# Float64 weights as one 24-bit word cut into short pieces, and the layer change's operands made by GpSimd

## The chip, the cores and the metric

The kernel runs on one core of a Trainium2 chip. A core has a matrix engine (TensorE, "PE" in the profile, its weight loads "PEld"), VectorE (DVE), ScalarE (ACT), GpSimd (POOL) and a queue engine (SP) that issues the loads here. Each engine runs its own instructions strictly in order and waits for others by semaphores. The metric is the device time of one execution in microseconds; the time before is the median of three runs.

## What is computed

Three stages follow each other: clustered attention, a feed-forward layer with ELU (layer 1) and a layer of four weighted experts with ReLU (layer 2).

```python
def reference(**kwargs):
    ...
    attn_out = _attn_ref(**attn_kwargs)            # 2 x 8 heads, 768 x 64, mask from 16 clusters
    x = attn_out.transpose(0, 2, 1, 3).reshape(1536, 512)
    x = _moe_ref(x=x, **moe_kwargs)                # h = x @ w_in;  ELU;  @ w_out   (512 -> 2048 -> 512)
    return _moe2_ref(x=x, **moe2_kwargs)           # out += p[:, e] * (relu(x @ w1[e]) @ w2[e]), e = 0..3
```

`w_in` and `w_out` arrive as float64 (divided by a square root in numpy), so the kernel reads them as pairs of 32-bit integers. All products are made in split form: each operand is a high part `h` and a low part `l`, and a product is `h*h + h*l + l*h`.

## The kernel before

**Attention** (the first 277 us) is a software pipeline written out by hand: the table `AT` gives each piece of work a time within a period, and sorting by time gives the order on every engine. The piece `W0` runs one step of `weights(n)`, which splits the float64 weights of chunks 0 and 1 of layer 1 in four halves (128x512, temporaries `w_tmp`), one step per period.

**Layer 1** has 16 weight chunks of 128 hidden features. A step is one chunk on one block of 512 tokens, so there are 48 steps (0 to 47), in groups of 2, 4, 5 and 5 chunks, each group over the three token blocks. In step s the main loop emits `tick(2s)`, then `emit_G1(s+2)` (12 matmuls from `xT` into PSUM `h`, then ACT relu and exp on L755 and L756, DVE `gg` on L757, POOL `gh` and `gl` on L758 and L759), then `tick(2s+1)`, then `emit_G2(s)` (12 matmuls on L869 into four PSUM banks `a`, of which there are five). Where a group closes (steps 1, 3, 5, 9, 13, 17, 22 and so on) the banks are moved into `acc` by ACT (L885, the first group) or added by DVE (L887). The next step's second bank can only be written when the first has been evicted. `tick` runs one piece (one `yield`) of each generator in `going`. The generator `w_split(n)` turns the float64 pair of chunk n (tile `st`) into `wh` and `wl`, starting at tick 4(n-2)-4 for chunks 2 to 14, so there is one chunk per two steps. Before, it has 7 DVE operations (L698, L702, L705, L709, L712, L717, L722), 2 of ACT (L701, L716) and one of POOL (L724, the last, which gives `wl`). Its temporaries are `wc` (two places in turn), `wql` and `wkh` (one place each, used by every chunk). Chunk 5 is first used by G1(9), the last first use of its group.

**Layer 2** has 16 chunks (16 to 31), 48 steps (48 to 95) and a Strassen-like product: `quad_early` makes five of seven products (the PSUM tile `px` is evicted by ACT on L779, L782 and L786 between its uses), then the first quarter of G2 of the step before, then `quad_late`, then the rest of G2. Its left operands are made by `x2_make` for each token block when layer 1 closes that block: four sums by DVE (`xs` on L828, L832, L838, L842) and seven splits, each an ACT copy (L645) and a subtraction by DVE (L648) or POOL (L650). Its right operands are made by `w2_split`: four differences `T` on DVE (L660 to L664) and five splits. The **layer change** is steps 47 to 51: block 2 closes in step 47, block 2's operands are first used by `quad_early(50)`, and chunk 17's by `quad_early(51)`. In the kernel before `ready` finishes a generator at the last moment, in front of the `quad_early` that needs it.

Of the kernel before, what the change touches and what calls it, by code (L numbers as in the profile page):

```python
# [46 lines left out]
def kernel(  # L47
# [56 lines left out]
    def attention():  # L104
# [379 lines left out]
        def weights(n):  # L484

            for i in range(2):
                raw = cv_p.tile([128, 512, 2], I32, tag="raw", name="w_raw")
                w_load(n, [raw], i)
                yield
                yield  # L490
                tmp = cv_p.tile([128, 3, 512], I32, tag="tmp", name="w_tmp")
                yield from w_split(n, [tmp[:, x] for x in range(3)], i)
# [159 lines left out]
    def w2_split(n):  # L652
# [3 lines left out]
        tags = W2_TAGS[n % 2]  # L656
        a = a.rearrange("p (k c f) -> p k c f", k=KD, c=2)
# [9 lines left out]
        for x, names in (  # L667
            (a[:, :, 0], ("B11", "B21")), (t[:, 0:2].rearrange("p a k f -> p (a k) f"), ("T1", "T2")),
            (t[:, 2:4].rearrange("p a k f -> p (a k) f"), ("T3", "T4")), (b22, ("B22",)),
        ):  # L670
            m = 2 * len(names)
            o = home(tags[len(ops) // 2], [128, 2, m, 128], "w1op")
            yield from split(o[:, 0], o[:, 1], x, dve)
            for i, nm in enumerate(names):
                ops[nm] = [[o[:, z, 2 * i + kk] for kk in range(2)] for z in range(2)]
            yield
        h, l = (home(tag, [128, 2, 512], "w2op") for tag in tags[4:])
        b = b.rearrange("p (c d) -> p c d", c=2)
        yield from split(h, l, b, dve)
# [3 lines left out]
    def w_split(n, tmp=None, half=None):  # L683
# [9 lines left out]

        small = tmp is not None
        c = tmp[0] if small else gtile(("qh", "kl")[n % 2], "wc", [128, 2, 512], I32)
        at = (slice(None),) * (len(a.shape) - 1)
        hi, lo = a[at + (1,)], a[at + (0,)]
        dve.tensor_scalar(c.bitcast(F32), hi.bitcast(F32), TOP, -TOP, ALU.min, ALU.max)  # L698
        yield
        b, s = tmp[1:] if small else [gtile(t, "w" + t, [128, 2, 512], I32) for t in ("ql", "kh")]  # L700
        act.activation(out=s.bitcast(F32), in_=c.bitcast(F32), func=AF.Abs)  # L701
        dve.tensor_scalar(b, c, 0x07FFFE00, 3, ALU.bitwise_and, ALU.logical_shift_left)  # L702
        if small:
            yield
        dve.scalar_tensor_tensor(  # L705
            out=b, in0=c, scalar=0xC0000000 - 2 ** 32, in1=b, op0=ALU.bitwise_and, op1=ALU.bitwise_or
        )
        yield
        dve.tensor_scalar(c, hi, 0x1FF, 23, ALU.bitwise_and, ALU.logical_shift_left)  # L709
        if small:  # L710
            yield
        dve.scalar_tensor_tensor(  # L712
            out=c, in0=lo, scalar=9, in1=c, op0=ALU.logical_shift_right, op1=ALU.bitwise_or
        )
        yield
        act.activation(out=c.bitcast(F32), in_=c.bitcast(U32), func=AF.Copy, scale=2.0 ** -43)  # L716
        dve.scalar_tensor_tensor(  # L717
            out=h, in0=s.bitcast(F32), scalar=LOW, in1=b.bitcast(F32), op0=ALU.is_ge, op1=ALU.mult
        )
        if small:  # L720
            yield
        dve.tensor_scalar(b, h.bitcast(I32), 0xFF800000 - 2 ** 32, None, ALU.bitwise_and)  # L722
        yield
        pool.tensor_tensor(l, c.bitcast(F32), b.bitcast(F32), ALU.mult)  # L724
        yield

    def moe():
# [84 lines left out]
        def x2_make(tb, t):  # L812
# [5 lines left out]
            def made(i, x):  # L818
                o = home(X2_TAGS[tb][i], [128, 2, 2, 256], "x2")
                x2[tb][i] = o[:, 0], o[:, 1]  # L820
                for _ in split(o[:, 0], o[:, 1], x, dve if i in (S1, S2, S4) else pool):
                    pass
# [89 lines left out]
        for n in range(W0, NC1):  # L912
            k = 5
# [6 lines left out]
        for n in range(NC1, NC1 + NP):  # L920
# [3 lines left out]
            else:  # L924
                t = 2 * (NS1 + NB * (i - 1)) + (1 if i > 1 else 2)
# [22 lines left out]
        for s in range(-LAG, NS):  # L948
# [11 lines left out]
            if s < NS1:  # L960
                tick(2 * s + 1)
            if s >= 0:
                emit_G2(s, (0,) if q else range(4))
            if q:
                quad_late(nxt, *q)
                if s >= NS1:
                    tick(2 * s, 3)
                    tick(2 * s + 1, 2)
# [37 lines left out]
```

## Time and profile before

| what | value |
|---|---|
| median of 3 runs | 1081.84 us (1081.2 to 1084.7) |
| profiled execution, its own time | 1085.26 us |
| its span, first to last instruction | 1083.4 us |
| PE busy | 1042.8 us (96%), 6253 matmuls |
| DVE, ACT, POOL busy | 781.2 us (72%), 495.3 us (46%), 396.7 us (37%) |
| attention | 0 to 276.9 us |
| layer 1 up to the first product of layer 2 | 276.9 to 557.4 us |
| layer change and layer 2 | 557.4 to 1083.4 us |
| granted TensorE clock, mean | 0.986 of full |

The shares are averages over stages with different limits: in attention DVE is busy for 95% of the time, in layer 2 for some 65%, and GpSimd does nothing in layer 2. PE's busy time contains stretches at half clock, and matmul ends are modelled, so a stage is judged by the pace of its steps and by PE's waits.

### The profile page before, as it was taken

Reading aid. Unit: us, or ns where it says so; the run is one execution under the profiler, and the core shown is the slowest. Engines: PE = TensorE matmul, PEld = TensorE weight load, DVE = VectorE, ACT = ScalarE, POOL = GpSimd, SP = SyncE. Lnnn points to the kernel's source line nnn. Section 1 sums busy time; section 2 is a strip of 40 time slices with the busy share of each in tenths; the row PEclk is TensorE's granted clock in tenths of the full one; section 3 lists DMA queues with packets and bytes.
Section 4 is the critical chain, followed back from the end, with each engine's and each line's share of the span. In section 5 each row is a group of like instructions: output and inputs, shape, how many; then the busy total and the mean of one; then the engine's idle time right before and its main releaser. Section 6 shows DMA issues by size and latency. Waiting matters only on the chain.

```text
span 1083.4 us, 16478 instructions
## 1 busy us (share of the span) xinstructions
PE 1042.8 (96%) x6253; PEld 927.2 (86%) x6253; DVE 781.2 (72%) x1305; ACT 495.3 (46%) x1045; POOL 396.7 (37%) x391
## 2 busy tenths in 40 slices
PE   8999999999988898999998999999999999999998
PEld 7989999988776776888887889899998989899997
DVE  6899999898788998342666676766566676666665
ACT  4888888888354333232434233333223333323331
POOL 2788788889666666453651000000000000000000
PEclk9899999999999999999999999999999999999999
DMA  8746554431123222110010111110111110011003
GB/s 182 171 106 154 139 133 107 108 89 51 67 82 113 79 78 78 39 39 1 1 39 1 39 40 40 39 39 2 39 40 40 40 40 20 20 40 40 1 1 117
DMA packets 61790, 67.53 MB, mean 62 GB/s; under 512 B 29008, under 2 KB 47440, under 8 KB 61712
## 3 DMA queue, kind: packets, MB, share of 16 engines
q1 hardware_dynamic: 61712, 66.49, 21.7%
q8 instruction: 49, 0.80, 0.3%
q14 instruction: 29, 0.24, 0.1%
HBM read 43.08 MB, written 3.15 MB: 43 GB/s over the span
## 4 chain that ended last, share of the span: by engine, by line
PE 61%; DVE 10%; POOL 5%; issue 2%; ACT 2%; POOLq 0%; DVEq 0%; ACTq 0%
PE a L869 30%; PE h L768 22%; PE h L748 6%; POOL wl L724 2%; DVE wql L705 2%; POOL gh L758 1%; PE x L441 1%; DVE wc L712 1%; DVE wql L702 1%; DVE wc L709 1%; DVE acc L887 1%; DVE gg L757 1%; PE tps L412 1%; POOL gl L759 1%; DVE wc L698 0%
## 5 line engine op out<-in xcount | busy, mean ns | idle before, releaser
L768 PEld LDWEIGHTS h<-x,w1op 128*128 128x128 f32 x2016 | 258.2, 191 | 14.9 <-ACT r L779 3.8
L768 PE MATMUL h<-x,w1op 128*128 128x256 f32 x2016 | 262.4, 285 | 5.2 <-ACT r L779 3.6
L869 PE MATMUL a<-w2op,gh 128*128 128x512 f32 x768 | 239.0, 392 | 0.0
L869 PEld LDWEIGHTS a<-w2op,gh 128*128 128x128 f32 x768 | 138.6, 189 | 24.0
L878 DVE SCALAR_TENSOR_TENSOR acc<-a,prob,acc 128x512 f32<-128x512 f32 x180 | 129.7, 746 | 40.2 <-PE a L869 40.2
L869 PE MATMUL a<-w2op,gl 128*128 128x512 f32 x384 | 150.1, 391 | 0.0
L748 PE MATMUL h<-xT,wh 128*128 128x512 f32 x384 | 120.3, 395 | 0.0
L400 POOL TENSOR_SCALAR p<-e,sm 128x768 f32<-128x768 f32 x96 | 90.4, 949 | 42.5 <-DVE sm L394 24.0
L373 DVE TENSOR_REDUCE nm<-s 128x1 f32<-128x768 f32 x96 | 90.8, 945 | 4.9 <-PE s L367 4.9
L869 PE MATMUL a<-gh,wh 128*128 128x512 f32 x192 | 76.8, 400 | 14.2 <-DVE acc L887 9.9
L382 ACT ACTIVATE e<-s,nm 128x768 f32<-128x768 f32 x96 | 86.7, 903 | 8.0 <-POOL p L400 6.1
L412 PE MATMUL tps<-ident,p 128*128 128x128 f32 x576 | 85.8, 280 | 3.6 <-DVE pl L433 3.1
L748 PEld LDWEIGHTS h<-xT,wh 128*128 128x128 f32 x384 | 73.6, 192 | 15.6
L869 PEld LDWEIGHTS a<-w2op,gl 128*128 128x128 f32 x384 | 72.3, 188 | 15.7
L758 POOL TENSOR_SCALAR gh<-gg 128x512 fp32r<-128x512 f32 x48 | 45.9, 956 | 108.6 <-DVE gg L757 102.5
L433 DVE TENSOR_TENSOR pl<-tps,ph 128x512 fp32r<-128x512 f32 x112 | 76.0, 682 | 6.0 <-ACT ph L425 5.4
L757 DVE SCALAR_TENSOR_TENSOR gg<-r,h 128x512 f32<-128x512 f32 x48 | 32.7, 681 | 65.4 <-ACT r L756 48.5
L779 ACT ACTIVATE r<-h 128x256 f32<-128x256 f32 x48 | 18.4, 384 | 131.6 <-PE h L768 131.6
L441 PE MATMUL x<-ph,v 128*128 128x256 f32 x288 | 76.7, 298 | 1.4 <-DVE xs L461 1.3
L748 PE MATMUL h<-xT,wl 128*128 128x512 f32 x192 | 75.5, 393 | 2.2 <-POOL wl L724 2.2
L869 PE MATMUL a<-gl,wh 128*128 128x512 f32 x192 | 76.3, 398 | 0.0
L869 PE MATMUL a<-gh,wl 128*128 128x512 f32 x192 | 76.2, 397 | 0.0
(152 smaller groups left out, 1916.3 us busy)
## 6 DMA issues: line engine op xcount, KB each, us to landing
st<-in_moe_w_dram SPq DMA_DIRECT2D x32, 512.0 KB, 4.3
st<-in_moe_w_in_dram SPq DMA_DIRECT2D x14, 512.0 KB, 3.8
st<-in_moe_w_out_dram SPq DMA_DIRECT2D x14, 512.0 KB, 4.6
QA<-qh SPq DMA_DIRECT2D x32, 192.0 KB, 3.9
nq<-in_q_dram SPq DMA_DIRECT2D x16, 192.0 KB, 3.8
nk<-in_k_dram SPq DMA_DIRECT2D x16, 192.0 KB, 3.8
nv<-in_v_dram SPq DMA_DIRECT2D x8, 384.0 KB, 4.0
QB<-ql SPq DMA_DIRECT2D x16, 192.0 KB, 3.8
```

The costliest lines, as they stand in the source:

```text
L373: dve.tensor_reduce(out=m_t[w][:, i:i + 1], in_=s_t[HALF * w + i][:, :, 0:384], axis=AX.XY, op=ALU.max, negate=True)
L382: act.activation(out=e, in_=s_t.pop(u)[:, :, 0:384], func=AF.Exp, bias=m_t[w][:, i:i + 1], accum_out=e_t[w][0][:, i:i + 1])
L400: pool.tensor_scalar(p, e_t[w][1 + i].rearrange("p a b -> p (a b)"), e_t[w][0][:, i:i + 1], 1.0, ALU.mult, ALU.mult)
L412: pe.transpose(ps[:, x, :], p_t[w][i][:, c * 128:(c + 1) * 128], ident)
L433: dve.tensor_tensor(out=l, in0=ps, in1=h.bitcast(F32), op=ALU.subtract)
L441: pe.matmul(x_t[w], lhsT=v2[j][:, r, c, :], rhs=t[:, :, c, :], start=(c == 0 and t is ph[w]), stop=(c == T - 1 and t is pl[w]),)
L748: pe.matmul(ps, lhsT=w[:, 0, f], rhs=x, start=(kk == 0 and i == 0), stop=(kk == KD - 1 and i == 2))
L757: dve.scalar_tensor_tensor(out=gg, in0=r, scalar=-1.0, in1=ps, op0=ALU.add, op1=ALU.max)
L758: pool.tensor_scalar(gh, gg, 1.0, 0.0, ALU.mult, ALU.add)
L768: pe.matmul(ps, lhsT=w[wz][kk], rhs=x[xz][:, kk], start=(start and kk + i == 0), stop=(stop and kk == 1 and i == 2), skip_group_check=True,)
L869: pe.matmul(ps, lhsT=x, rhs=y, start=(opens and i == 0), stop=(closes and i == len(ops) - 1))
L878: dve.scalar_tensor_tensor(out=t, in0=ps, scalar=pr, in1=t, op0=ALU.mult, op1=ALU.add)
```

## The change

`w_split` is written anew. The absolute value of the high word is taken by ACT, clamped between `LOW` and `TOP` by DVE, shifted by DVE, joined with three bits of the low word by DVE; ACT takes the sign of the high word and once more an absolute value (which clears the top bit), DVE multiplies by the sign; then an ACT copy gives `h` and a POOL subtraction gives `l`. That is 4 operations of DVE, 4 of ACT and 1 of POOL, in 6 ticks instead of 5 (8 steps in attention, as before). The temporaries are `wa` (two places in turn) and `wsg` (one place); nothing of it is read by POOL except `wa` and `wh`. `tick(2s+1)` now stands behind `emit_G2(s)`, so behind a group's evictions. At the layer change, block 2's seven splits and chunk 17's five are subtracted by POOL, four pieces of block 2's `x2_make` run right behind step 47, and chunk 17 starts two ticks earlier.

```diff
@@ weights (attention)
-                tmp = cv_p.tile([128, 3, 512], I32, tag="tmp", name="w_tmp")
-                yield from w_split(n, [tmp[:, x] for x in range(3)], i)
+                tmp = cv_p.tile([128, 2, 512], I32, tag="tmp", name="w_tmp")
+                yield from w_split(n, [tmp[:, x] for x in range(2)], i)
@@ w2_split
+        eng = pool if n == NC1 + 1 else dve
...
-            yield from split(o[:, 0], o[:, 1], x, dve)
+            yield from split(o[:, 0], o[:, 1], x, eng)
...
-        yield from split(h, l, b, dve)
+        yield from split(h, l, b, eng)
@@ w_split
-        c = tmp[0] if small else gtile(("qh", "kl")[n % 2], "wc", [128, 2, 512], I32)
+        a32, sg = tmp if small else [gtile(("qh", "kl")[n % 2], "wa", [128, 2, 512], I32), gtile("ql", "wsg", [128, 2, 512], I32)]
...
-        dve.tensor_scalar(c.bitcast(F32), hi.bitcast(F32), TOP, -TOP, ALU.min, ALU.max)
+        x, sg = a32.bitcast(F32), sg.bitcast(F32)
+        act.activation(out=x, in_=hi.bitcast(F32), func=AF.Abs)
         yield
-        b, s = tmp[1:] if small else [gtile(t, "w" + t, [128, 2, 512], I32) for t in ("ql", "kh")]
-        act.activation(out=s.bitcast(F32), in_=c.bitcast(F32), func=AF.Abs)
-        dve.tensor_scalar(b, c, 0x07FFFE00, 3, ALU.bitwise_and, ALU.logical_shift_left)
+        dve.tensor_scalar(x, x, LOW, TOP, ALU.max, ALU.min)
         if small:
             yield
+        dve.tensor_scalar(a32, a32, 3, 0x40000000, ALU.logical_shift_left, ALU.bitwise_xor)
+        act.activation(out=sg, in_=hi.bitcast(F32), func=AF.Sign)
+        yield
         dve.scalar_tensor_tensor(
-            out=b, in0=c, scalar=0xC0000000 - 2 ** 32, in1=b, op0=ALU.bitwise_and, op1=ALU.bitwise_or
+            out=a32, in0=lo, scalar=29, in1=a32, op0=ALU.logical_shift_right, op1=ALU.bitwise_or
         )
         yield
-        dve.tensor_scalar(c, hi, 0x1FF, 23, ALU.bitwise_and, ALU.logical_shift_left)
+        act.activation(out=x, in_=x, func=AF.Abs)
+        yield
+        dve.tensor_tensor(out=x, in0=x, in1=sg, op=ALU.mult)
+        yield
+        act.activation(out=h, in_=x, func=AF.Copy)
         if small:
             yield
-        dve.scalar_tensor_tensor(
-            out=c, in0=lo, scalar=9, in1=c, op0=ALU.logical_shift_right, op1=ALU.bitwise_or
-        )
-        yield
-        act.activation(out=c.bitcast(F32), in_=c.bitcast(U32), func=AF.Copy, scale=2.0 ** -43)
-        dve.scalar_tensor_tensor(
-            out=h, in0=s.bitcast(F32), scalar=LOW, in1=b.bitcast(F32), op0=ALU.is_ge, op1=ALU.mult
-        )
-        if small:
-            yield
-        dve.tensor_scalar(b, h.bitcast(I32), 0xFF800000 - 2 ** 32, None, ALU.bitwise_and)
-        yield
-        pool.tensor_tensor(l, c.bitcast(F32), b.bitcast(F32), ALU.mult)
+        pool.tensor_tensor(l, x, h.bitcast(F32), ALU.subtract)
         yield
@@ x2_make
-                for _ in split(o[:, 0], o[:, 1], x, dve if i in (S1, S2, S4) else pool):
+                for _ in split(o[:, 0], o[:, 1], x, dve if i in (S1, S2, S4) and tb < NB - 1 else pool):
@@ moe, the plan and the main loop
-            k = 5
+            k = 6
...
-                t = 2 * (NS1 + NB * (i - 1)) + (1 if i > 1 else 2)
+                t = 2 * (NS1 + NB * (i - 1)) + (i > 1)
...
-            if s < NS1:
-                tick(2 * s + 1)
             if s >= 0:
                 emit_G2(s, (0,) if q else range(4))
+            if s < NS1:
+                tick(2 * s + 1, 4 if s == NS1 - 1 else 1)
...
-                    tick(2 * s, 3)
+                    tick(2 * s, 4 if s == NS1 else 3)
```

**What moves on the engines.** First, VectorE in layer 1, over the two steps that one chunk takes. `gg` is a step's eviction; all else is the weights of a chunk (`wh4` is chunk 4's high part). Before:

```order
L757 SCALAR_TENSOR_TENSOR gg_4622<-r_4621,h_4606 128x512
L702 TENSOR_SCALAR wql_4628<-wc_4601 128x1024
L705 SCALAR_TENSOR_TENSOR wql_4628<-wc_4601,wql_4628 128x1024
L709 TENSOR_SCALAR wc_4601<-st_4508 128x1024
L712 SCALAR_TENSOR_TENSOR wc_4601<-st_4508,wc_4601 128x1024
L757 SCALAR_TENSOR_TENSOR gg_4668<-r_4667,h_4652 128x512
L717 SCALAR_TENSOR_TENSOR wh4_4599<-wkh_4629,wql_4628 128x1024
L722 TENSOR_SCALAR wql_4628<-wh4_4599 128x1024
L698 TENSOR_SCALAR wc_4696<-st_4603 128x1024
```

and now, for the same chunk:

```order
L755 SCALAR_TENSOR_TENSOR gg_4613<-r_4612,h_4597 128x512
L705 TENSOR_SCALAR wa_4591<-wa_4591 128x1024
L708 TENSOR_SCALAR wa_4591<-wa_4591 128x1024
L711 SCALAR_TENSOR_TENSOR wa_4591<-st_4501,wa_4591 128x1024
L755 SCALAR_TENSOR_TENSOR gg_4658<-r_4657,h_4642 128x512
L717 TENSOR_TENSOR wa_4591<-wa_4591,wsg_4592 128x1024
L755 SCALAR_TENSOR_TENSOR gg_4706<-r_4705,h_4690 128x512
```

Three of the seven operations are gone, and three stand behind one step's `gg` and one behind the next.

Second, GpSimd around step 8 of layer 1. `gh` and `gl` belong to a step's G1, and `wl5` is chunk 5's low part. Before, from G1(7)'s pair on:

```order
L758 TENSOR_SCALAR gh_4760<-gg_4763 128x512
L759 TENSOR_TENSOR gl_4761<-gg_4763,gh_4760 128x512
L724 TENSOR_TENSOR wl5_4695<-wc_4696,wql_4723 128x1024
L758 TENSOR_SCALAR gh_4809<-gg_4812 128x512
L759 TENSOR_TENSOR gl_4810<-gg_4812,gh_4809 128x512
L758 TENSOR_SCALAR gh_4854<-gg_4857 128x512
```

and now, again from G1(7)'s pair on:

```order
L756 TENSOR_SCALAR gh_4748<-gg_4751 128x512
L757 TENSOR_TENSOR gl_4749<-gg_4751,gh_4748 128x512
L756 TENSOR_SCALAR gh_4796<-gg_4799 128x512
L757 TENSOR_TENSOR gl_4797<-gg_4799,gh_4796 128x512
L722 TENSOR_TENSOR wl5_4683<-wa_4684,wh5_4682 128x1024
L756 TENSOR_SCALAR gh_4840<-gg_4843 128x512
```

`wl5` has gone one step back: it stood between the pairs of G1(7) and G1(8) and stands now between those of G1(8) and G1(9), and G1(9) reads it.

Third, ScalarE at the layer change. L779 (now L777) is the first eviction of a `quad_early`, L809 (now L807) the last of a `quad_late`, `x2` are block 2's operands, made from `acc` and the sums `xs`. Before, from step 49's last eviction to step 50's first:

```order
L809 ACTIVATE gh_6633<-c_6583 128x512
L645 ACTIVATE x2_6656<-acc_4732 128x512
L645 ACTIVATE x2_6661<-xs_6654 128x512
L645 ACTIVATE x2_6664<-xs_6659 128x512
L645 ACTIVATE x2_6669<-acc_4732 128x512
L645 ACTIVATE x2_6674<-xs_6667 128x512
L645 ACTIVATE x2_6698<-acc_4732 128x512
L645 ACTIVATE x2_6701<-xs_6672 128x512
L779 ACTIVATE r_6707<-h_6704 128x256
```

Now four of the seven stand one step earlier, from step 48's last eviction to step 49's first:

```order
L807 ACTIVATE gh_6500<-c_6459 128x512
L645 ACTIVATE x2_6548<-acc_4716 128x512
L645 ACTIVATE x2_6553<-xs_6546 128x512
L645 ACTIVATE x2_6556<-xs_6551 128x512
L645 ACTIVATE x2_6561<-acc_4716 128x512
L777 ACTIVATE r_6567<-h_6564 128x256
```

The other three follow at the old place, with two copies of chunk 17's operands (`w1op`, the second from the differences `T`) in front of step 50's first eviction:

```order
L807 ACTIVATE gh_6619<-c_6569 128x512
L645 ACTIVATE x2_6642<-xs_6559 128x512
L645 ACTIVATE x2_6648<-acc_4716 128x512
L645 ACTIVATE x2_6653<-xs_6640 128x512
L645 ACTIVATE w1op_6656<-st_6451 128x512
L645 ACTIVATE w1op_6659<-T_6645 128x512
L777 ACTIVATE r_6686<-h_6683 128x256
```

So the work between two steps' evictions is split over two places; on GpSimd the twelve subtractions (seven of `x2`, five of chunk 17) stand in one row where four of `x2` stood.

## Rows read from the trace of the kernel before

**Rows 1.** Chain of waits, full-speed stretch of layer 1: start, us, engine, operations.

```profile
440.65 2.72 PE a L869 x12
443.37 2.72 PE h L748 x12
```

**Rows 2.** Timeline, PE: start, us, operation, count, idle before and its releaser.

```profile
557.45 3.78 PE L768 MATMUL h<-x,w1op 128*128 128x256 f32 x30
...
568.07 3.84 PE L768 MATMUL h<-x,w1op 128*128 128x256 f32 x30
...
578.68 1.95 PE L768 MATMUL h<-x,w1op 128*128 128x256 f32 x12
584.22 3.24 PE L768 MATMUL h<-x,w1op 128*128 128x256 f32 x18 [3.59 <-ACT r L779]
...
597.59 0.62 PE L768 MATMUL h<-x,w1op 128*128 128x256 f32 x3 [1.52 <-DVE w1op L648]
```

**Rows 3.** Waits of PE's matmuls in layer 1: total us, times, longest.

```profile
PE a L869 <- DVE acc L887: 9.9, 4, 4.4
...
PE a L869 <- ACT acc L885: 4.2, 2, 3.6
...
PE h L748 <- POOL wl L724: 2.2, 1, 2.2
```

**Rows 4.** Busy time by stretch: length, PE, PEld, DVE, ACT, POOL, clock, DMA, GB/s.

```profile
276.93:557.45 280.52, 264.11 (x1131) 215.40 (x1129) 195.89 (x206) 105.03 (x156) 165.86 (x117) 0.98 0.17 57
557.45:608.00 50.55, 45.34 (x272) 40.39 (x271) 32.81 (x56) 16.59 (x36) 9.16 (x8) 0.97 0.07 22
326.00:338.00 12.00, 9.76 (x44) 7.74 (x43) 10.14 (x10) 4.94 (x7) 7.94 (x6) 1.00 0.24 82
100.00:160.00 60.00, 57.27 (x439) 53.84 (x438) 56.78 (x102) 52.88 (x122) 49.62 (x58) 1.00 0.52 121
```

**Rows 5.** Timeline, DVE, layer 1.

```profile
281.18 0.69 DVE L757 SCALAR_TENSOR_TENSOR gg<-r,h 128x512 f32<-128x512 f32 x1 [2.48 <-ACT r L756]
...
282.50 1.51 DVE L705 SCALAR_TENSOR_TENSOR wql<-wc,wql 128x1024 int32<-128x1024 int32 x1
284.12 1.59 DVE L709 TENSOR_SCALAR wc<-st 128x1024 int32<-128x1024 int32 x1
...
293.73 1.10 DVE L702 TENSOR_SCALAR wql<-wc 128x1024 int32<-128x1024 int32 x1 [1.72 <-POOL wl L724]
```

**Rows 6.** Timeline, POOL, layer 1.

```profile
282.02 0.92 POOL L758 TENSOR_SCALAR gh<-gg 128x512 fp32r<-128x512 f32 x1 [2.25 <-DVE gg L757]
283.03 2.13 POOL L759 TENSOR_TENSOR gl<-gg,gh 128x512 fp32r<-128x512 f32 x1
...
440.31 2.40 POOL L724 TENSOR_TENSOR wl<-wc,wql 128x1024 fp32r<-128x1024 f32 x1
```

**Rows 7.** Groups of instructions by form: count, busy us, mean ns, idle before.

```profile
L701 ACT ACTIVATE wkh<-wc 128x1024 f32<-128x1024 f32 x14 | 14.8, 1059 | 21.9 <-DVE wc L698 21.7
...
L650 POOL TENSOR_TENSOR x<-xs,x 128x512 fp32r<-128x512 f32 x3 | 3.9, 1290 | 0.0
...
L167 ACT ACT_TABLE_LOAD x1 | 1.3, 1283 | 0.7 <-PEq L990 0.7
```

**Rows 8.** Busy time of `w_tmp`'s instructions in attention: DVE, ACT, POOL.

```profile
44.00:248.00 204.00, 21.72 (x28) 5.08 (x8) 5.11 (x4) 1.00 0.49 116
```

**Rows 9.** Chain of waits in attention.

```profile
221.44 1.00 DVE w_tmp L709
```

**Rows 10.** Timeline, DVE, layer change.

```profile
566.24 2.73 DVE L887 TENSOR_TENSOR acc<-a,acc 128x512 f32<-128x512 f32 x4 [0.90 <-PE a L869]
...
576.54 1.79 DVE L828 TENSOR_TENSOR xs<-acc 128x512 f32<-128x512 f32 x1
```

**Rows 11.** Timeline, ACT, layer change.

```profile
579.70 0.62 ACT L645 ACTIVATE x<-acc 128x512 fp32r<-128x512 f32 x1
...
583.81 0.36 ACT L779 ACTIVATE r<-h 128x256 f32<-128x256 f32 x1
```

## The prediction

> **What bounds the kernel now.** I read the chain of waits first. From 277 us on it goes almost wholly through PE at full speed: twelve matmuls take 2.72 us in either product of layer 1 [rows 1]. So layer 1 has a floor. From its first matmul to the first product of layer 2, 48 blocks of G1 and 46 of G2 run, 94 x 2.72 = 255.7 us, and the stretch took 280.5 [rows 4]. The 24.8 us between are what this change can win there. 16.3 of them are waits of the matmuls [rows 3]: 14.1 for an accumulator bank that DVE or ACT had not evicted, 2.2 for `wl5`. The rest, 8.5, is PE running slowly: the mean granted clock is 0.98 there [rows 4], that is, it falls to the 1.2 GHz level for some microseconds behind long waits. So a microsecond of waiting brought half of one in slow running.
>
> Why are evictions late? In the cycle from 326 to 338 DVE is busy for 10.1 of 12 us while PE is busy for 9.8 [rows 4]: a chunk's seven operations (8.8 us) and two `gg` fill it, and the evictions queue behind them. The reader should see that the cycle is closed by the temporary `wql`: DVE's L702 waits for the last chunk's `wl` [rows 5], POOL makes that behind `gh` and `gl`, and those wait for DVE. Also, DVE and POOL hold each other up: `gh` ends at 282.94, and the DVE operation issued beside it ends 1.07 later; `gl` ends 1.15 after that, and the next DVE operation 0.55 after `gl` [rows 5, 6]. They run in turn.
>
> Layer 2 is PE's own from about 608 on. At the layer change PE waits 3.59 us for ACT's eviction behind seven `x2` copies, and 1.52 us for chunk 17's operands [rows 2].
>
> **Part 1, attention.** The weights of chunks 0 and 1 cost DVE 21.7 us in 28 operations and ACT 5.1 us in 8 [rows 8]. The change takes 12 DVE operations of some 0.78 us away (9.3 us) and adds 8 of ACT at 0.63 (5.1 us); the number of steps (8 a half) and their places stay. DVE is busy for 56.8 of 60 us in this stage, ACT for 52.9, PE for 57.3 [rows 4], and weight operations do stand on the chain of waits [rows 9]. If all of DVE's saving counted the gain would be 9.3; if none did and ACT's work lay on the path, a loss of 5. I take 3 us of gain, a third of DVE's saving, since PE, with 57.3 of 60, lies just above.
>
> **Part 2, layer 1.** DVE goes from seven operations a chunk to four: two single-input, two with two inputs, 0.55 to 1.6 and 1.1 to 1.5 each [rows 5], 3.3 to 6 us, with two `gg` (0.69 each) at most 7.4 in the 10.9 us of two steps at full speed. ACT's four cost 4 x 1.06 [rows 7], and with its relu and exp of two steps it stays under 7. POOL's pairs, free of DVE 0.92 + 1.15 each, and `wl`, 2.4 [rows 6], are 6.5. No temporary waits for POOL's `wl` any more before two chunks later. In turn DVE (3.2) and POOL (6.5) need 9.7 of each 10.9, so PE becomes the bound, with little to spare; and evictions stand in front of the weights' pieces instead of behind them. So all 24.8 us go, but for what is late next. That is `wl5`. It now stands behind the pair of G1(8) and G1(9) reads it. From the start of G1(0)'s `gg` (281.18), which is 1.53 after G1(0)'s last issue (276.93 + 2.72), `gh` took until 1.76 [rows 5, 6]; then in turn the second DVE operation 0.55, `gl` 1.15, the third DVE operation 1.07 and `wl` 2.4 [rows 6]: 6.9. `wl5` is ready 8.4 us after G1(8)'s last issue. PE gets there after G2(6) and two matmuls, 2.72 + 0.45 = 3.2. A wait of 5.2 us (4.1 if `wl` goes ahead of the third DVE operation, 5.8 if one more DVE operation of 0.55 goes ahead of it). At half a microsecond each, slow running adds 2.7. The same sum for chunk 4, which has one step more, gives 8.4 against 8.6: no wait. Layer 1 keeps 7.9 of 24.8 us lost: **a gain of 16.9** (13 to 20).
>
> **Part 3, the layer change.** Four `x2` pieces now stand in front of step 49's evictions. Block 2's bank adds end at 568.97 [rows 10]. POOL's first subtraction needs only the first two banks, starts about 568.4 and takes 1.29 [rows 7]; DVE's first sum waits for it, as at 576.54 where it took 1.79 [rows 10], and ends about 570.2. From there to the fourth copy's end took 2.0 before (578.33 to 580.32 [rows 10, 11]), so step 49's first eviction starts at 572.1 and PE goes on at 572.5; by 584.22 against 583.81 that takes 0.4 [rows 2, 11]. PE was due at 568.07 + 12 x 0.12 = 569.5 [rows 2]: 3.0 us of new wait. Step 50 then starts at 578.68 + 3.0 = 581.7. In front of its first eviction stand three copies and two of chunk 17, the last of which needs three DVE operations behind the third `x2` sum (a sum and three differences, two inputs each). POOL has five subtractions of 1.29 at hand in the same 6 us. In turn: the sum at 581.3, then POOL 1.25 and DVE 0.35 alternately three times to 586.1, the copy to 586.8, PE on at 587.1. Due 581.7 + 1.4 = 583.1: 4.0 us. If they did not take turns the differences would be done by 582.8, and this would be 0.9.
>
> The Trainium skill (SBUF — State Buffer, section "SBUF: two separate sides") states that a DVE operation with two SBUF inputs and a GpSimd operation share a port pair as an exclusive lock, held for the whole instruction. The trace's turns above agree, and by that rule the wait is 4.0 and not 0.9.
>
> Chunk 17 is then in time for step 51. So waits of 7.0 us with 2.2 of slow running (1.9 by this stage's old ratio, 3.5 by layer 1's) stand for the old 4.1 (578.68 + 1.4 to 584.2), 1.6 and 1.5 of slow running (0.03 x 50.55 [rows 2, 4]): **2.0 us worse**, from 3.3 better to 4 worse. The last of POOL's twelve subtractions, of 0.8 to 2.4 us, hide behind layer 2's products, where POOL has nothing else to do; without that cover they are the last three's 4.5 us.
>
> **Sum.** -3.0 - 16.9 + 2.0 = -17.9. Against the profiled execution: 1085.26 (span 1083.4, 1.9 around it) becomes 1067.4, span 1065.5. That execution was 3.4 above the median; against 1081.84, **1064**. With all terms at their ends (attention -9 to +5, layer 1 -20 to -13, the change -3.3 to +4) it would be 1049 to 1078.
>
> **Rivals.**
> *The port binds.* If turn-taking costs more than I count (three of DVE's four at the contended 1.5 [rows 5], one at 0.55, and POOL's 6.5), a chunk's cycle is 11.6 and not 10.9; 13 cycles lose 9, with the 8 for `wl5` 17 of 24.8: gain 3 + 8 - 2 = 9, 1073. For it: 9.7 of 10.9 us is little margin. Against: DVE's stretch of three ends before the next `gg`.
> *The layer change goes well.* If DVE slips through between POOL's operations and no clock falls there, part 3 is 3.0 + 0.9 - 7.2 = -3.3; with 5 in attention, 1057.
> *Slower.* The weights become one serial chain through three engines: relu, exp, `gg`, `gh`, `gl` of both steps (3.8 each) with `wl` and the DVE operations in between (6.2), 13.8 us a chunk. Twelve chunks then lose 12 x 2.9 = 35, with the clock 40, against 24.8: 1081.8 - 3 + 2 + 15 = 1096. It decides from 12.9 us a chunk on. Against: PSUM `h` and the temporaries have two places, so steps overlap.
> *Sign costs table loads.* A load took 1.28 us [rows 7]. Two for each of 18 `Sign`s: 10 us in attention, where ACT has 12% free, and 2.6 a chunk in layer 1, where ACT's 6.7 + 2.6 + bank copies pass 10.9 in the cycles that close a group, which I put at 7 us: 1081.8 + 7 - 10 + 2 = 1081, no change. Against: both programs hold two loads, none by `Sign`.
> The Trainium skill (ScalarE: Activation LUTs, section "Table sets: the hidden batching unit") names relu, copy, identity and abs as found in every set, not sign, next to exp. By that a switch could be needed; the trace has no `Sign` to show it.
> *It doesn't do what it says.* Two pieces hold two engines (shift with `Sign`, copy with subtraction). `Sign` reads only the loaded word; the subtraction waits for its copy, 1.06 us on ACT [rows 7] beside the pair that POOL makes first. So this costs nothing by itself.
>
> **How the numbers follow.** Forecast 0.60, port 0.16, layer change well 0.13: faster 0.89. No change: table loads 0.03, smaller losses that cancel 0.02: 0.05. Slower 0.06. 0.3% is 3.2 us, about what a measurement of this kernel tells from no change. The range for 8 in 10 is 1053 to 1076: it takes in the port's 1073 and the other's 1057, with 3 to 4 us each for their sizes, and leaves out no change and slower.
>
> **What would show it.** In layer 1: no wait for an eviction, blocks of 2.72 throughout, one wait of about 5 us for `wl5` at G1(9) with the clock's fall behind it, first product of layer 2 near 538 (557.45 - 16.9 - 3). DVE cycles under 8 us busy. At the change: a wait of 2 to 3 for ACT at step 49, one of 1 to 4 at step 50, none at step 51. Attention's end near 274. Wrong would be: waits for `gl` or `gh` on PE in each cycle (port or chain), or a later end of attention (ACT).

## The result and the profile after

The changed kernel takes 1068.97 us (median, 1067.4 to 1069.8) beside 1083.27 us of the kernel before on the same chip: a ratio of 0.9868, 95% interval 0.9844 to 0.9891, that is 14.3 us less. Measured a second time beside the experiments it was 1067.78 for 1084.59, 0.9851 (0.9829 to 0.9874), 16.8 us less. The forecast was 1064 and 17.9 us less, with a range of 1053 to 1076. One execution of experiment e5 took 2613 us where its other four took 1058 to 1064, and no ratio below contains it.

The profiled executions differ by 15.4 us (span 1083.4 and 1068.0). By stage: the first matmul of layer 1 at 274.54 for 276.93 (2.4 us less), layer 1 to the first product of layer 2 in 263.16 for 280.52 (17.4 less), layer change and layer 2 in 530.3 for 525.95 (4.4 more).

Busy time by stretch of the kernel after (columns as in [rows 4]): layer 1, the 50.55 us from the first product of layer 2 on, 12 us of layer 1, and the 60 us of attention that [rows 4] has of before.

```profile
274.54:537.70 263.16, 258.17 (x1130) 213.25 (x1129) 151.04 (x164) 132.91 (x184) 163.14 (x118) 0.99 0.18 61
537.70:588.25 50.55, 44.36 (x255) 39.97 (x254) 29.26 (x45) 16.70 (x36) 19.76 (x15) 0.90 0.06 21
...
392.00:404.00 12.00, 12.00 (x55) 9.94 (x54) 7.83 (x7) 6.58 (x8) 9.86 (x7) 1.00 0.26 89
...
100.00:160.00 60.00, 59.21 (x461) 56.99 (x460) 56.13 (x105) 55.38 (x129) 52.82 (x62) 1.00 0.54 132
```

Against [rows 4]: in layer 1 VectorE is busy for 151 us, not 196. The 12 us that [rows 4] shows of layer 1 hold a wait for `wl5`, so they are no measure for the 12 us above; over the same microseconds the kernel before had:

```profile
392.00:404.00 12.00, 11.05 (x49) 8.82 (x48) 11.67 (x12) 3.52 (x5) 7.70 (x6) 1.00 0.26 88
```

There PE is now busy for all 12 us, before 11.05, and DVE for 7.8, before 11.7. In attention PE gets to 59.2 of 60 us, before 57.3. Only behind 537.70 has it become worse: clock 0.90, before 0.97.

Waits of PE's matmuls in the kernel after (total us, times, longest), which answer [rows 3] and the waits in [rows 2]:

```profile
PE h L766 <- ACT r L777: 6.2, 2, 3.3
PE h L746 <- POOL wl L722: 5.0, 1, 5.0
```

The 14.1 us of waits for accumulator banks are gone. What is left is one wait for `wl5` in layer 1 and two for ACT at the layer change. The chain of waits of the kernel after, around the first (start, us, engine, tile and line):

```profile
304.66 2.72 PE a L867 x12
307.38 2.72 PE h L746 x12
...
316.96 0.70 DVE gg L755
...
317.81 0.93 POOL gh L756
...
318.82 1.58 POOL gl L757
320.39 3.29 POOL wl L722
...
323.73 4.63 PE h L746 x10
328.36 2.79 PE a L867 x12
```

The reader should see blocks of 2.72 up to the wait, then G1(8)'s pair and `wl5` in a row on GpSimd, and behind it ten matmuls in 4.63 us that take 2.27 at full speed. The two engines take turns here as the prediction drew it up; VectorE's side of the same microseconds (timeline):

```profile
318.29 0.98 DVE L708 TENSOR_SCALAR wa<-wa 128x1024 int32<-128x1024 int32 x1
319.31 2.16 DVE L711 SCALAR_TENSOR_TENSOR wa<-st,wa 128x1024 int32<-128x1024 int32 x1
```

L708 ends at 319.27, `gl` 1.13 later at 320.40, L711 1.07 after `gl`, and `wl5` 2.2 after L711. The Trainium skill (SBUF — State Buffer, section "SBUF: two separate sides") states that a VectorE operation with two SBUF inputs and a GpSimd operation that reads SBUF exclude each other for a whole instruction; L711 has two inputs, and this row of ends agrees. L708 has one input and took its turn here too, ending 0.53 us behind `gh`.

PE at the layer change, kernel after (timeline; steps 48, 49 and 50):

```profile
537.70 3.78 PE L766 MATMUL h<-x,w1op 128*128 128x256 f32 x30
...
548.33 1.59 PE L766 MATMUL h<-x,w1op 128*128 128x256 f32 x12
552.80 3.60 PE L766 MATMUL h<-x,w1op 128*128 128x256 f32 x18 [2.89 <-ACT r L777]
...
563.49 1.59 PE L766 MATMUL h<-x,w1op 128*128 128x256 f32 x12
568.38 4.21 PE L766 MATMUL h<-x,w1op 128*128 128x256 f32 x18 [3.30 <-ACT r L777]
```

Against [rows 2]: one wait of 3.59 at step 50 and one of 1.52 at step 51 have become 2.89 at step 49 and 3.30 at step 50. That is 1.1 us more of waiting. The other 3.3 of the 4.4 lie in the granted clock. Busy time by stretch behind each of the three waits (the column before the last two is the clock): the kernel after, then the same kernel in its second profile, then experiment e1, whose layer change is the same.

```profile
320.00:330.00 10.00, 6.28 (x18) 5.01 (x19) 1.71 (x2) 1.57 (x3) 3.67 (x2) 0.66 0.30 105
552.00:558.00 6.00, 5.20 (x25) 4.86 (x26) 2.60 (x3) 1.83 (x5) 3.37 (x3) 0.72 0.00 0
566.00:574.00 8.00, 5.62 (x22) 5.33 (x23) 4.65 (x7) 1.97 (x5) 2.39 (x2) 0.58 0.01 2
```

```profile
320.00:330.00 10.00, 6.72 (x23) 5.46 (x24) 2.18 (x3) 2.67 (x4) 3.71 (x2) 0.83 0.30 105
548.00:556.00 8.00, 5.11 (x28) 4.82 (x27) 4.13 (x5) 2.76 (x7) 4.94 (x4) 0.79 0.00 0
563.00:575.00 12.00, 8.70 (x49) 7.85 (x49) 8.33 (x13) 2.99 (x8) 4.25 (x4) 0.86 0.00 1
```

```profile
544.00:552.00 8.00, 5.11 (x37) 4.66 (x37) 5.08 (x7) 3.46 (x8) 4.40 (x4) 1.00 0.00 0
558.00:570.00 12.00, 8.81 (x53) 7.91 (x54) 9.39 (x15) 4.77 (x10) 5.01 (x5) 1.00 0.00 1
```

The missing share of the clock times the length is what the stretch lost to the 1.2 GHz level: 0.34 x 10 = 3.4, 0.28 x 6 = 1.7 and 0.42 x 8 = 3.4 us in the first profile; 0.17 x 10, 0.21 x 8 and 0.14 x 12, each 1.7, in the second; nothing at the layer change of e1. The waits in front are the same to 0.01 us. So a fall of the clock is worth 1.7 us, or twice that where it lasts, and how often it falls behind the same wait differs between executions of one program. The executions without a profile agree: e1's four took 1053.88 to 1061.77 us, with mean granted clocks of 0.997 to 0.991.

### The profile page after: what moved, and what is told of

Same layout as the page of the kernel before. It is cut to its first block, busy times and chain, and to the rows that moved or that the text cites. A ratio compares the mean times of both kernels' runs of the same rounds, so it can differ in the third digit from the quotient of the medians.

```text
span 1068.0 us, 16450 instructions
## 1 busy us (share of the span) xinstructions
PE 1036.9 (97%) x6253; PEld 927.0 (87%) x6253; DVE 730.0 (68%) x1243; ACT 526.4 (49%) x1081; POOL 400.7 (38%) x399
## 4 chain that ended last, share of the span: by engine, by line
PE 85%; DVE 5%; POOL 4%; ACT 3%; issue 2%; DMA 1%; SPq 1%; ACTq 0%; POOLq 0%; DVEq 0%
PE a L867 36%; PE h L766 23%; PE h L746 12%; PE x L441 4%; PE tps L412 3%; PE s L364 2%; PE s L367 2%; POOL p L400 1%; DVE pl L433 1%; DVE nm L373 1%; ACT e L382 1%; ACT ph L425 1%; PE qkps L199 1%; PE lps L240 1%; PE lps L239 1%
## 5 line engine op out<-in xcount | busy, mean ns | idle before, releaser
L777 ACT ACTIVATE r<-h 128x256 f32<-128x256 f32 x48 | 18.4, 384 | 129.6 <-PE h L766 129.6
L753 ACT ACTIVATE r<-h 128x512 f32<-128x512 f32 x48 | 28.6, 597 | 106.9 <-PE h L746 106.1
L756 POOL TENSOR_SCALAR gh<-gg 128x512 fp32r<-128x512 f32 x48 | 40.6, 846 | 94.9 <-DVE gg L755 94.9
```

Source lines behind the costliest of these rows:

```text
L756: pool.tensor_scalar(gh, gg, 1.0, 0.0, ALU.mult, ALU.add)
```

## The experiments

Each kernel was timed beside the kernel before. The stages below are those of the profiled executions; "waits" are PE's, "falls" what the clock cost, summed over short stretches as above; all in us.

| kernel | first matmul of layer 1 | layer 1 | its waits | its falls | from layer 2's first product | waits at the change | falls there |
|---|---|---|---|---|---|---|---|
| before | 276.9 | 280.5 | 16.3 | 6.8 | 525.9 | 5.1 | 1.7 |
| after | 274.5 | 263.2 | 5.0 | 3.4 | 530.3 | 6.2 | 5.1 |
| after, again | 274.1 | 262.5 | 5.0 | 1.7 | 529.4 | 6.2 | 3.4 |
| e1, chunk 5 early | 274.3 | 257.7 | 1.4 | 0 | 525.2 | 6.2 | 0 |
| e2, change undone | 274.9 | 262.9 | 5.0 | 3.4 | 524.1 | 3.6 | 1.7 |
| e3, pieces before | 273.7 | 262.9 | 5.0 | 1.7 | 528.2 | 6.2 | 3.4 |
| e4, old word behind | 277.6 | 274.8 | 12.8 | 5.1 | 522.8 | 3.6 | 0 |
| e5, T early | 273.4 | 263.1 | 5.0 | 3.4 | 523.7 | 2.9 | 1.7 |
| e6, by VectorE | 273.5 | 263.0 | 5.0 | 3.4 | 526.9 | 4.6 | 3.4 |
| e7, all three | 274.7 | 256.6 | 0.3 | 0 | 521.3 | 2.3 | 0 |
| e8, attention old | 279.0 | 263.8 | 5.0 | 3.4 | 528.0 | 6.2 | 3.4 |
| e9, change alone | 277.6 | 279.6 | 13.3 | 10.2 | 530.0 | 6.5 | 5.1 |

The table adds up. Take waits and falls off the last stage and 518.4 to 519.8 stays in all twelve profiles; off layer 1, 254.5 to 257.4, where twelve matmuls in 2.72 us give a floor of 255.7. (A fall that begins inside a wait costs less than its count, up to 1 us, which is why some lie below the floor.) So in both stages the time is a floor, the waits and the falls, within 2 us.

**e1, chunk 5 one tick earlier.**

```diff
-            t += 4
+            t += 3 if n == 4 else 4
```

> The changed kernel, but chunk 5's weights start one tick earlier (three ticks behind chunk 4's start, not four), so that wl5 stands in front of G1(8)'s pair on GpSimd. My theory: all that layer 1 still loses (263.2 us for a floor of 255.7) is the one wait for wl5, 5.0 us, and the 2.4 us of slow running behind it. Then the wait falls to under 1 us, the stretch from the first product of layer 1 to the first of layer 2 to 256 to 257 us, and the time by 6.5 to 7.5 us, to about 1062. Rival, the port or the serial chain binds: chunks 4 and 5 get in each other's way, wl4 or a pair gl is late instead, and 2 to 4 us remain of the wait: time lower by 2 to 4. Rival, the clock falls there without a wait: 2.4 stay, time lower by 5.

It took 1059.23 us, a ratio of 0.9756 (0.9726 to 0.9786). Waits of PE's matmuls:

```profile
PE h L766 <- ACT r L777: 6.2, 2, 3.3
...
PE h L746 <- POOL wl L722: 1.4, 2, 1.1
```

The wait of 5.0 is gone; 1.1 appear at `wl4` in G1(8), since ScalarE's `Sign` of chunk 5 now waits 1.36 us for chunk 4's multiplication, which reads the one place of `wsg`, and a `relu` stands behind it. Layer 1 takes 257.7 us. So the wait and the falls behind it were what layer 1 still lost (2.0 us over its floor are left, 1.4 of them waits), and no port and no chain binds behind it. The time fell by more than expected, 8.7 us between this profile and the second one of the changed kernel: 3.6 of waits, 1.7 of falls in layer 1, and 3.4 of falls at the layer change, which this edit doesn't touch.

**e2, the layer change undone.** Block 2 and chunk 17 as before, with one piece behind step 47.

```diff
-        eng = pool if n == NC1 + 1 else dve
+        eng = dve
...
-dve if i in (S1, S2, S4) and tb < NB - 1 else pool
+dve if i in (S1, S2, S4) else pool
...
-                t = 2 * (NS1 + NB * (i - 1)) + (i > 1)
+                t = 2 * (NS1 + NB * (i - 1)) + (1 if i > 1 else 2)
...
-                tick(2 * s + 1, 4 if s == NS1 - 1 else 1)
+                tick(2 * s + 1)
...
-                    tick(2 * s, 4 if s == NS1 else 3)
+                    tick(2 * s, 3)
```

> The changed kernel with the layer change as it was before (seven x2 splits of block 2 and chunk 17's splits as before on VectorE and GpSimd, one piece behind step 47, chunk 17 two ticks later). My theory, from the two traces: the new layer change costs 6.5 of waits and 4.5 of slow running, the old one 5.7 and 1.7, so this kernel is 3.5 to 4.5 us faster than the changed one, about 1065, with the old waits of 3.6 at step 50 and 1.5 at step 51. The forecast on record: 2.0 faster, 1067. Rival: the slow running at the change belongs to the place and not to the two waits; then it stays and the time falls by under 1.5. Second rival: the layer change was worth something and this is slower than the changed kernel.

It took 1062.73 us, 0.9796 (0.978 to 0.9811): faster than the changed kernel's second measurement by 5.1 us (the intervals don't meet), more than the 3.5 to 4.5 expected. PE at the change:

```profile
562.70 3.49 PE L766 MATMUL h<-x,w1op 128*128 128x256 f32 x18 [2.07 <-ACT r L777]
...
576.03 2.90 PE L766 MATMUL h<-x,w1op 128*128 128x256 f32 x22 [1.52 <-DVE w1op L648]
```

Step 51's wait is the old one, step 50's is 1.5 us shorter than the 3.59 of before: the one piece behind step 47 brings that (e4, which has this piece too, shows the same 2.07), without a wait at step 49, where the changed kernel's four pieces make one of 2.9. The waits are 2.6 less than in the changed kernel, the falls 1.7 to 3.4 less.

**e3, the changed kernel with the pieces in front of the evictions again.**

```diff
+            if s < NS1 - 1:
+                tick(2 * s + 1)
             if s >= 0:
                 emit_G2(s, (0,) if q else range(4))
-            if s < NS1:
-                tick(2 * s + 1, 4 if s == NS1 - 1 else 1)
+            if s == NS1 - 1:
+                tick(2 * s + 1, 4)
```

> The changed kernel, but the second piece of each step (tick 2s+1) stands in front of G2(s) and its evictions again, as before; the four pieces behind step 47 stay. Theory A, VectorE's load was the cause in layer 1 and the place matters little: the odd pieces now hold 1.7 us of VectorE's work that is ready early, so the evictions wait 0 to 3 us in all, and the time is 1069 to 1073. Theory B, the place behind the evictions was the cause: the 14.1 us of waits for evictions come back for the most part, with slow running, 1079 to 1088.

It took 1064.94 us, 0.9813 (0.9793 to 0.9832), below the 1069 to 1073 of theory A. No wait for a bank came back; waits of PE's matmuls:

```profile
PE h L766 <- ACT r L777: 6.2, 2, 3.3
PE h L746 <- POOL wl L722: 5.0, 1, 5.0
```

These are the changed kernel's. The place behind the evictions is worth nothing once the word is short; that it was even a little faster (its interval and that of the changed kernel's second measurement just meet) is in no wait, and falls of the clock alone differ by that much from one execution to the next.

**e4, the kernel before with its pieces behind the evictions.**

```diff
-            if s < NS1:
-                tick(2 * s + 1)
             if s >= 0:
                 emit_G2(s, (0,) if q else range(4))
+            if s < NS1:
+                tick(2 * s + 1)
```

> The kernel before, with nothing changed but that the second piece of each step stands behind G2(s) and its evictions. Theory A, VectorE's load was the cause: the evictions are on time, but the weights then are late, since a chunk's cycle still takes about 12 us where two steps at full speed take 10.9; waits for evictions turn into waits for wl or gl, and the time is 1076 to 1086. Theory B, the place was the cause: layer 1 gains most of the 14.1 us of waits and their slow running, 1062 to 1070.

It took 1076.48 us, 0.992 (0.9904 to 0.9937). Waits of PE's matmuls, and the busy time of the cycle of [rows 4]:

```profile
PE a L869 <- DVE acc L887: 5.7, 3, 3.2
PE h L748 <- POOL wl L724: 4.2, 1, 4.2
...
PE h L748 <- DVE wh L717: 1.7, 1, 1.7
```

```profile
326.00:338.00 12.00, 7.84 (x28) 6.07 (x29) 10.15 (x10) 3.74 (x5) 7.91 (x6) 0.72 0.25 86
```

VectorE is as full as before (10.15 of 12 us). Theory A expected the evictions on time; the waits for banks fall from 14.1 to 5.7, and 7.1 of waits for weights and `gg` stand where 2.2 stood. Layer 1 takes 5.7 us less than before, so with the old word the place alone brings a third of the 17.4 us. With e3 this settles the cause in layer 1: the new word brings the whole gain by itself, and the place adds nothing to it.

The word relieves VectorE in two ways that no run parts: it has three operations fewer, and none of them waits for GpSimd's `wl` any more. In the kernel before VectorE stood still for that (waits of VectorE; the kernel after has no such row):

```profile
DVE wql L702 <- POOL wl L724: 15.1, 9, 1.7
```

Which of the two the evictions needed is therefore open.

**The changed kernel again**, beside e5 to e7, unaltered.

> The changed kernel once more, unaltered, beside the others of this set. My theory of the clock: the falls behind the three waits (5.0 at G1(9), 2.9 at step 49, 3.3 at step 50) differ from execution to execution, each fall costing 1.7 us, and the waits do not; so the waits are again 5.0, 2.9 and 3.3 to 0.1 us, and the time is 1062 to 1069 with 1 to 5 falls. Rival: the falls belong to the waits; then there are again two behind the first, one behind the second and two behind the third, and 1068 to 1070.

1067.78 us. The waits were again 5.00, 2.89 and 3.30, the falls 5.1 us in all and not 8.5, as the rows above show. So the waits belong to the program, and the number of falls differs between its executions; the rival, two, one and two falls again, is out.

**e5, chunk 17's differences early.**

```diff
+            if t == 2 * NS1 - 6:
+                going.append(w2_split(NC1 + 1, True))
...
-load_at.setdefault(t - (8 if i == 0 else 4), []).append(n)
+load_at.setdefault(t - (8 if i == 0 else 12 if i == 1 else 4), []).append(n)
```

`w2_split(n, True)` makes the four differences and ends; the later generator passes two empty pieces in their place.

> The changed kernel, but chunk 17's four differences T are made by VectorE six ticks earlier (and its load twelve ticks ahead, not four); their places in chunk 17's row of pieces stay empty, so ScalarE's and GpSimd's orders are the same. Theory: the wait of 3.3 us at step 50 is the copy from T, which waits for differences of 1.5 us each that take turns with GpSimd. Then the copy follows its neighbour at once, and the wait at step 50 is 0.2 to 0.6; step 49's 2.9 stays; the time falls by 2.8 and by up to 3.4 of slow running, to 1060 to 1066. Rival: the five copies in front of the eviction are the wait, whatever T does; then 2 us or more stay, and the time falls by under 1.3.

It took 1062.63 us (median of the four), 0.98 (0.9772 to 0.9827). In the changed kernel the copy from `T` had waited on VectorE (timelines of the kernel after, VectorE and ScalarE):

```profile
563.07 1.51 DVE L661 TENSOR_TENSOR T<-st 128x256 f32<-128x256 f32 x1
564.50 1.49 DVE L662 TENSOR_TENSOR T<-st 128x256 f32<-128x256 f32 x1
565.92 1.48 DVE L664 TENSOR_TENSOR T<-T,st 128x256 f32<-128x256 f32 x1
```

```profile
567.43 0.63 ACT L645 ACTIVATE w1op<-T 128x512 fp32r<-128x512 f32 x1 [3.10 <-DVE T L664]
567.97 0.37 ACT L777 ACTIVATE r<-h 128x256 f32<-128x256 f32 x1
```

Each of these three differences takes 1.5 us; the fourth, with no GpSimd operation beside it, took 0.42. With `T` early ScalarE's row closes up (its lines have moved by ten), and PE goes through step 50 without a wait:

```profile
562.49 0.61 ACT L645 ACTIVATE w1op<-st 128x512 fp32r<-128x512 f32 x1
563.01 0.62 ACT L645 ACTIVATE w1op<-T 128x512 fp32r<-128x512 f32 x1
563.53 0.36 ACT L787 ACTIVATE r<-h 128x256 f32<-128x256 f32 x1
```

So the step-50 wait was the differences, as forecast, and not the number of copies.

**e6, the splits by VectorE as before, all pieces in the changed kernel's places.**

```diff
-        eng = pool if n == NC1 + 1 else dve
+        eng = dve
...
-dve if i in (S1, S2, S4) and tb < NB - 1 else pool
+dve if i in (S1, S2, S4) else pool
```

> The changed kernel, but the splits S1, S2 and S4 of block 2 and the five of chunk 17 are subtracted by VectorE as before; all pieces keep their places. Theory, GpSimd's eight additional subtractions cost by turns: step 49's wait stays at 2.9 (its first sum waits for a GpSimd subtraction that was there before too), step 50's falls from 3.3 to 2.0 to 2.8, since GpSimd has two subtractions left there that take turns with the differences; the time is 0.5 to 2 lower. Rival, GpSimd takes work off VectorE: the five subtractions of 0.7 to 1.2 us on VectorE delay the differences or the evictions, step 50 or 51 waits longer, and the time is 1 to 3 higher.

It took 1065.23 us, 0.9814 (0.9785 to 0.9843). VectorE's differences and PE at step 50:

```profile
562.50 1.51 DVE L661 TENSOR_TENSOR T<-st 128x256 f32<-128x256 f32 x1
563.94 0.41 DVE L662 TENSOR_TENSOR T<-st 128x256 f32<-128x256 f32 x1
564.28 0.41 DVE L664 TENSOR_TENSOR T<-T,st 128x256 f32<-128x256 f32 x1
```

```profile
565.68 3.92 PE L766 MATMUL h<-x,w1op 128*128 128x256 f32 x18 [1.74 <-ACT r L777]
```

One difference of 1.5 us is left, and the wait falls from 3.30 to 1.74. Giving the splits to GpSimd costs these 1.6 us of waiting. The 1.74 lie below the 2.0 to 2.8 expected. The time alone decides nothing here, since its interval overlaps with the changed kernel's.

**e7, all three waits taken away.** e1 with a second place for `wsg`, e5 without the empty pieces, and another order for block 2: behind step 47 the three pieces A11 (with the sum s1), A12 (with s2) and A22, whose copies need no sum; behind step 48's `quad_late` S1, S2 (with s4), S4 (with s3) and S3. Beside the edits of e1 and e5:

```diff
-dve if i in (S1, S2, S4) and tb < NB - 1 else pool
+dve if i in (S1, S2, S4) else pool
...
-gtile("ql", "wsg", [128, 2, 512], I32)
+gtile(("ql", "kh")[n % 2], "wsg", [128, 2, 512], I32)
...
-                tick(2 * s + 1, 4 if s == NS1 - 1 else 1)
+                tick(2 * s + 1, 3 if s == NS1 - 1 else 1)
```

> A version that takes away all three waits of the changed kernel: chunk 5 one tick earlier and two places for wsg; T early without empty pieces; behind step 47 only the three copies of block 2 that need no sum (A11, A12, A22), the sums and the S copies behind step 48's quad_late, with S1, S2 and S4 subtracted by VectorE. If the three waits and the falls of the clock behind them are all that is lost, layer 1's stretch is 256 to 257 us, the waits at steps 49 to 51 are under 0.6 each, and the time is 1069 - 7.4 - 6.2 less up to 5 of slow running, 1050 to 1056. Rival: another wait takes their place at the change (the S copies now crowd in front of step 50's eviction with three of chunk 17): 2 us there, 1054 to 1060.

It took 1053.99 us, 0.9722 (0.9697 to 0.9746), the fastest of all. Layer 1, and PE at steps 49 and 50:

```profile
274.71:531.31 256.60, 256.27 (x1131) 211.57 (x1129) 149.67 (x167) 131.64 (x184) 163.22 (x117) 1.00 0.18 62
```

```profile
544.35 2.43 PE L773 MATMUL h<-x,w1op 128*128 128x256 f32 x18 [0.81 <-ACT r L784]
...
556.60 2.43 PE L773 MATMUL h<-x,w1op 128*128 128x256 f32 x18 [1.48 <-ACT r L784]
```

Layer 1 is within a microsecond of its floor. At the change 2.3 us stay, more than the 0.6 each that was hoped for, and no fall of the clock behind them. So the rival's new wait of 2 us did come; the time is inside the theory's range, at the lower edge of the rival's.

**e8, the old word in attention alone** (`w_split` of before for the four halves of chunks 0 and 1, the new one in layer 1).

```diff
-                tmp = cv_p.tile([128, 2, 512], I32, tag="tmp", name="w_tmp")
-                yield from w_split(n, [tmp[:, x] for x in range(2)], i)
+                tmp = cv_p.tile([128, 3, 512], I32, tag="tmp", name="w_tmp")
+                yield from w_split_old(n, [tmp[:, x] for x in range(3)], i)
```

> The changed kernel, but the four halves of chunks 0 and 1 are split in attention by the old word (seven VectorE operations, two of ScalarE and one of GpSimd each, in the same eight steps); layer 1 and the layer change as in the changed kernel. Theory: attention's gain is the 12 VectorE operations, so the first product of layer 1 goes back from 274 (eight profiles of the new word: 273.4 to 274.9) to 277 (two profiles of the old one: 276.9 and 277.6), and all behind it is as in the changed kernel, with the wait of 5.0 for wl5: 2.5 to 3.5 slower than that, 1070 to 1073. Rival: attention's difference is chance of the clock and of the loads; the start of layer 1 stays at 274 to 275 and the time within 1.5.

It took 1071.29 us, 0.9876 (0.9854 to 0.9898), and layer 1 began at 279.0, 2 us later than expected. The intervals of the whole times overlap with the changed kernel's, so the time alone doesn't decide it. The first column of the table does: the four profiles with the old word there have 276.9 to 279.0, the eight with the new one 273.4 to 274.9, and the means are 3.7 us apart.

**e9, the layer change alone**, on the kernel before: the pieces of e2's diff the other way round, with four pieces behind step 47.

> The kernel before with the layer change of the changed kernel alone (four pieces of block 2 behind step 47, chunk 17 two ticks earlier, its five splits and block 2's seven on GpSimd); old word and old order of pieces elsewhere. Theory: the waits at the change are those of the changed kernel, 2.9 at step 49 and 3.3 at step 50, none at step 51, for 3.6 and 1.5 before: 1.1 us more of waits, and one or two falls of the clock of 1.7 more or less; layer 1 as before, 280 to 281. Time 1 to 4 above the kernel before. Forecast on record: 2.0 above. Rival: the layer change brings something that the changed kernel hides, and this is 1 or more below the kernel before.

It took 1087.73 us, 1.0036 (1.0023 to 1.0049): slower than the kernel before by 3.6 us in the medians (1084.14) and by 3.9 in the ratio. PE at steps 49 and 50:

```profile
572.65 3.28 PE L769 MATMUL h<-x,w1op 128*128 128x256 f32 x18 [3.24 <-ACT r L780]
...
588.24 2.08 PE L769 MATMUL h<-x,w1op 128*128 128x256 f32 x8 [3.30 <-ACT r L780]
```

Waits of 6.5 for 5.1, and falls of 5.1 for 1.7. This part makes the kernel slower by itself, as e2 said from the other side.

## Why the prediction was right, and where it was off

**Direction and mechanism** were right: faster, through layer 1, with `wl5` and the two evictions of the layer change late next. The time came out 3.6 us above the forecast's difference in the first measurement and 1.1 in the second.

**Attention, forecast 3.0 less.** The profiles of before and after say 2.4, the twelve together 3.7, e8 that it comes from the word. VectorE's saving itself was 8.1 us and not 9.3 (its 21.72 us of weights [rows 8] became 13.61), ScalarE's addition 5.5. A third of the saving came close, led by the stage's PE row, 57.27 of 60 us; but the third was chosen between a loss of 5 and a gain of 9.3, not worked out, so this hit is in part luck. (VectorE's 95% in attention, which stands ahead, is that of 100 to 160 us; over the whole stage it was 88%, 244.8 of 277 us.)

**Layer 1, forecast 16.9 less, 17.4 measured.** The floor of 94 x 2.72 us is what e7 reaches to 0.9. No wait for a bank is left, as said, and e3 with e4 show the reason that was given (VectorE is relieved by the word) and not the one that the order of the pieces suggests; fewer operations and the temporary that no longer waits for `wl`, both of which the prediction named, stay together. The wait for `wl5` was put at 5.2 and is 5.0, and its sum (two operations' turns, `gl`, a third, `wl`: 6.9 us) is met link by link: 316.96 to 323.67 is 6.7. The slow running behind it was put at 2.7; in the seven profiles that have this wait the stage less floor and wait leaves 1.8 to 3.1, 2.4 in the mean. That this came close is luck too, since the same kind of ratio failed at the layer change. Chunk 4 was in time, as said, by a hair: e1, in which a `relu` comes 2.3 us later, makes it late by 1.1.

**The layer change, forecast 2.0 worse; 3.6 to 3.9 by e9, 4.4 by the profiles**, which is outside this part's own range (to 4 worse). The waits were right: step 49 put at 3.0, measured 2.89 behind the modelled ends; step 50 put at 4.0, measured 3.30, with the turns that e5 and e6 confirm (1.41 us each and not 1.6); step 51 none. The term that was mis-sized is the "2.2 of slow running (1.9 by this stage's old ratio, 3.5 by layer 1's)". It was 5.1 and 3.4 in the changed kernel's two profiles, and 0 to 5.1, mean 3.4, in the six profiles that have this layer change. A ratio of slow running to waiting was the wrong form. What the rows show is a number of falls, each worth 1.7 us: none or one behind each wait of 2.1 us at the change (e2, e4), none or one behind each of 2.9, none to two behind each of 3.3, none behind those of 0.8 to 1.5 there, one behind the 1.74 of e6. One long wait and a short one had become two long ones, and the forecast should have counted two chances for a fall, not 7.0 us times a ratio.

**The rivals.** *The port binds* is out: layer 1 less waits and falls stands at the floor. *The layer change goes well* is out: both waits are there. *One serial chain* is out: outside the one wait, blocks run at 2.72. *It doesn't do what it says* is out at the one place that waited: the copy that gives chunk 5's `wh` ended at 317.81, and `wl5` began at 320.36, behind `gl`. *Sign's table loads* are out; the groups of ScalarE in the kernel after hold the two loads of before, none by `Sign`:

```profile
L167 ACT ACT_TABLE_LOAD x1 | 1.3, 1283 | 0.7 <-PEq L988 0.7
...
L526 ACT ACT_TABLE_LOAD x1 | 1.3, 1283 | 0.0
```

**What stays open.** What decides how often the clock falls behind a given wait was not tried; the runs show only that equal waits are followed by different numbers. Nor is it shown whether layer 1 needed the three operations fewer or the end of VectorE's waits for `wl`.

## What to carry to other kernels

When PE is the floor, count each stage as floor, waits and falls of the clock; if the three don't add up to the stage, something is still unseen. When an engine is full, taking work from it helps more than moving it behind what is urgent: here the place alone left 12.8 of 16.3 us of waits (14.1 for banks became 5.7, but 2.2 of others became 7.1). Before work goes to GpSimd, look whether VectorE has two-input operations on the critical path at that moment: here GpSimd's row of subtractions beside them made three differences of 0.42 us take 1.5 each, and with two subtractions fewer there (e6) one did.

## What the runs showed of the hardware

Behind the same waits (2.89 and 3.30 us, equal to 0.01) the granted clock fell to the 1.2 GHz level for a loss of 5.1, 3.4, 3.4, 3.4 and 0 us in five profiles (after, after again, e3, e8, e1), always in portions of 1.7. One edit in layer 1 (e1) can so seem to gain 3.4 us in a stage that it doesn't touch. A difference of that size between two kernels needs its waits compared before it is believed.
